# A new fixed order for the same 1440 tasks in a fused attention and MLP kernel on one core

## The chip, the core and the metric

The kernel runs on one core of a Trainium2 chip. Five engines work side by side, each through its own list of instructions in order: TensorE (PE) multiplies, with its weight loads shown as PEld; VectorE (DVE), ScalarE (ACT) and GpSimd (POOL) do the element work; SyncE (SP) issues most transfers. The metric is the device time of the kernel in microseconds, as the median of several executions. One execution is also recorded by the hardware profiler, and all durations below come from that record.

## The reference

One layer on x of shape 1 × 2048 × 640 in bfloat16: a normalisation without weights, attention with 32 heads of 20 columns over four segments of 512 tokens with a memory carried from one segment to the next, the output product and the residual, then a second normalisation and an MLP with 1728 hidden columns.

```python
q, k, v = (heads(layernorm(x) @ w) for w in (wq, wk, wv))   # B, 32, 4, 512, 20
phi = lambda t: jnp.where(t > 0, t + 1.0, jnp.exp(t))
for s in range(4):
    logits = qs @ ks.T * 20 ** -0.5 + causal_mask
    a_dot = softmax(logits) @ vs
    a_mem = (phi(qs) @ M) / (phi(qs) @ z + 1e-06)
    o = sigmoid(beta) * a_mem + (1.0 - sigmoid(beta)) * a_dot
    M = M + phi(ks).T @ vs
    z = z + phi(ks).sum(over tokens)
h = x + o @ wo
h2 = h + silu(layernorm(h) @ w1) @ w2
```

## The kernel before, in words

The 2048 tokens are sixteen blocks of 128, four blocks to a segment. Heads are taken four at a time, so a segment has eight groups, called ticks; the ticks are numbered 0 to 31 over the four segments. A function declares every piece of work as a named task with the buffers that it reads and writes. Which engine runs it, which buffer it gets and in which order the tasks are issued is then read from one long string, ORDER.

The names in ORDER, with s the segment, c a group of columns, k a tick and b a block:

- `n1_st`, `n1_rs`, `n1_ap`, `n1_tr` (b): statistics of the first normalisation on VectorE (lines 720 and 723), the reciprocal root on GpSimd (729, 731), the application on VectorE (737), the transpose by a transfer on SP (761). Blocks 0 to 3 are transposed by TensorE instead (`n1_tp`, line 746) and copied out by ScalarE or VectorE (`n1_te`, 755 and 756). `n2_` names the same for the second normalisation.
- `re_wq`, `re_wk` (c): the raw weights A_wq and A_wk copied into the column order that the heads need, in two or three pieces each, on ScalarE (693), VectorE or GpSimd (695).
- `pr` s c w: the projection for queries (w is 0) or keys (1), in two parts, `.0` with two products and `.1` with three, of 512 columns each; `qe` copies it out of PSUM (830, 831). `v` s i: the values, five products of 320 columns in each half; `ve` copies them out (797, 798).
- `ex`, `pa`, `pb`: the feature map phi (837, 844, 850). `kt`, `mz`, `ma`, `mb`: the memory's update (transpose by a transfer, products at line 1057, sum at 1083 and 1086, mask at 1093). `vt`: transfers that gather the remaining columns of the heads for groups 5 to 7.
- `qk` k with a, b or e: score products (line 900); `e` k: their exponentials on ScalarE (913), two instructions of 128 × 1024 for each; `mk` k: the causal mask on GpSimd (925). `av` k: the product with the values (948); `oe` its scaling (961, 963); `tn` k: back to token order with the memory's part (977, 981); `nm` k: the division (994 and 996, or 1008, 1013 and 1014); `ad` k: the sum of the two parts on GpSimd (1022).
- `ot` b: transpose by a transfer (1110); `wo` b: output product in two halves; `rs` b: the residual (1125). `h1_` s f: the first MLP product, again in parts with two and three products; `th` and `s`: the activation on ScalarE (1160) and VectorE (1166). `h2_` b q: the second MLP product in four parts; `o` b: the last residual (1202); `out` b: the store (1207). `x`, `w_`, `beta`: loads (578, 581, 590).
- `mt`, `mta`, `mtb`, `mm`, `mzc`, `zf`, `lsc`, `epsg`, `vpad`, `iota`, `sel`, `warm`, `fill`: constants and products that only keep TensorE busy at the start.

An entry reads `name/engine:slots`. The letter is A, D, G or S for ScalarE, VectorE, GpSimd or SyncE, where a task has a choice; `/C` on a TensorE task means that each product, whose weights are 128 columns wide, is issued as four products of 32 columns on four parts of the array (line 546 in the profile instead of 545). The array is thus used in three layouts: full (most products), four row parts (scores) and four column parts (av, `/C`, the short last part of h1). The slots are the buffers that the task takes: for TensorE tasks, PSUM banks 0 to 7, of which scores take two pairs at a time. A bank can be given anew when every task of its former owner stands earlier in the list.

A tracker then turns the list into five instruction streams. Each engine gets its own tasks in list order; semaphores are added where a task needs another engine's result, and where it writes to a buffer that another engine still has to read. So the list sets the order on every engine and also, through the slots, who waits for whose buffers. The function that reads the list:

```python
for row in ORDER:
    name, _, slots = row.partition(":")
    name, _, eng = name.partition("/")
    ...
    t.cols = eng == "C"
    t.eng = {"A": AC, "D": DV, "G": PO, "S": SP, "C": PE}[eng] if eng else list(t.engs)[0]
    ...
            a.slot = slots.pop(0)
```

Of the kernel before, what the change touches and what calls it, by code (L numbers as in the profile page):

```python
# [327 lines left out]
D = 640  # L328
# [34 lines left out]
zpad:0 iota epsc vpad1 mt0 x0:0 mta0 mtb0 halfc sel mt3 n1_st0:6 x1:1 n1_rs0 n1_st1:1 x2:2 x3:3 w_q:0 n1_st2:3 n1_rs1  # L363
n1_rs2 n1_st3:5 fill20:0 n1_rs3 re_wq0/G:0 re_wq1/G n1_ap1:0 n1_ap2:2 mm2 w_k mt1 warm:0 re_wk1/G:0 fill9:0 n1_tp1:4
mm9 re_wk2/G n1_ap0:3 n1_ap3:0 w_wv:0 n1_tp2:2 n1_tp0:0 mm6 n1_tp3:6 n1_te3/D:2 vpad0 mta3 beta n1_te1/A n1_te2/A mta1
re_wq2/G n1_te0/A re_wk0/A x4/A:4,5,6,7 mtb3 re_wk3/G pr000.0:6 pr000.1 qe000/A:0 pr010.0:1 pr001.0:2 re_wk4/A pr001.1
qe001/D pr011.0:7 pr011.1 zf0 zf1 mm8 qe011/D:0 pa011:1 re_wq3/G qk0a0:4,2 lsc0 lsc1 x8/A:8,9,10,11 ex001:1 re_wq4/G
pa001:2 pb001 kt00:0 mzc9 e0a0:4 pr010.1 qe010/D e0a2 mtb1 pr021.0:7 pr021.1 qe021/D:0 n1_st4:4 n1_rs4 v00.0:6 pa021:0
ex011:2 qk0b0:3,1 e0b0:5 e0b2 mk0b w_w1_3/S:0 w_w1_4/S pb011 v01.0:0 mm1 n1_st5:5 v00.1 ve00/A:0 pr020.0:5 pr020.1
qe020/A v01.1 n1_rs5 vt09:0 ex021:1 vt03 w_w2_5/S qk0e0:2,6 e0e2:0 v02.0:4 v02.1 v03.0:6 e0e0 n1_st6:6 ve01/D ve02/A  # L370
n1_st9:1 qk1a0:2,0 n1_ap5:2 n1_rs6 v03.1 n1_ap6:0 e1a0:1 pr031.0:4 pr031.1 kt01:1 n1_tr5:0 vt00 e1a2 n1_tr6 ve03/D
qk1b0:2,5 e1b0:6 e1b2 pb021 qe031/D:0 w_w1_0/S pr030.0:7 pr030.1 n1_ap4:3 n1_tr4 pr041.0:4 mk1a qk2a0:2,0 n1_st10:3
lsc2 mzc6 pa031:1 qe030/D pr041.1 qe041/D:0 ex031:1 pr040.0:5 pr040.1 vt06 e2a2:3 qe040/D vt08 vt04 e2a0 qk2b0:6,0
e2b0:2 vt07 lsc3 mk0e mk1b mz00:4 mk0a ma00/D:0 pb031 vt02 n1_rs10 av1:3 e2b2 oe1/D:1 mm5 mm11 mzc5 av0:2 oe0/D:0 mm0
qk2e0:4,6 e2e0:6 mz01:0 ma01/D:2 tn0:2 qk3a0:4,0 e2e2 mt2 e3a2:0 nm0:1,0 tn1:3 nm1:1 v10.0:2 v10.1 mk2b n1_st7:5
ve10/D:1 kt02:0 e3a0 mk2a n1_st11:6 qk3b0:0,6 mk2e vt05 e3b2:1 n1_rs7 e3b0 vt01 av2:5 oe2/D:1 mm3 mk3a qk4a0:6,2
mz02:4 ma02/D:3 mk3b v11.0:0 e4a2:2 vt010 e4a0 qk4b0:2,4 n1_rs9 mta2 mm4 n1_ap7:3 n1_st8:5 n1_rs8 kt03:1 e4b0:4 e4b2
vt011 v11.1 ve11/D mk4b tn2:7 nm2:1 pa041:2 mz03:6 ex041:2 qk4e0:2,0 e4e0:3 av3:7 e4e2 mk4a n1_tr7 epsg0 pr100.0/C:4
pr100.1/C ma03/D:4 oe3/D:0 qk5a0:2,6 mzc1 e5a0:5 mk4e pr110.0:5 pb041 e5a2 kt04:0 qe100/D:0 pr110.1 pr120.0:4
qe110/D:0 qk5b0:2,0 pa110:0 mtb2 av4:5 oe4/D:1 pa100:0 pr120.1/C mzc2 n1_ap10:3 n1_tr10:2 e5b2:6 qk6a0:0,6 w_w1_1/S  # L380
mz04:5 qe120/D:0 e5b0 ma04/D:1 v12.0:2 tn3:4 nm3:2 n1_ap8:1 e6a2:4 v12.1 ve12/D e6a0 tn4:7 ex100:1 pb100 nm4:2
qk6b0:4,0 pr101.0:6 e6b2:0 mk5b pr101.1 e6b0 qk6e0:0,2 e6e2:1 mk5a av5:7 n1_rs11 pa120:0 mzc0 e6e0 pr111.0/C:4 qe101/D
w_w2_3/S pr111.1/C qk7a0:2,5 e7a0:3 e7a2 n1_ap9:3 oe5/D:0 pr130.0:7 n1_tr8 qe111/D tn5:0 pa111:2 mm7 v13.0:4 nm5:2
pr130.1 qe130/D:0 qk7b0:2,0 mzc7 mzc3 mb01:0 mk6b v13.1/C ex111:1 pb111 mk6e mk6a av6:6 n1_tr9 mzc4 ve13/D e7b2:5
pr140.0/C:7 pr140.1/C qk8a0:0,4 pa101:1 oe6/D:0 pr121.0:6 pr121.1 e7b0 qe140/D:0 tn6:7 ex101:2 ex120:0 pb101 mb02:0
pb120 e8a0:4 mk7b e8a2 qk8b0:2,0 w_wo/S:0 e8b2:0 e8b0 mk7a qe121/D av7:6 nm6:0 pr131.0/C:7 oe7/D:1 kt10:1 qk8e0:0,4
e8e2:6 tn7:6 pa130:0 kt11:0 nm7:0 pr131.1/C qe131/D e8e0 mz11:2 ma11 qk9a0:5,3 mzc8 pr141.0:7 w_w2_4/S n1_ap11:3
vt10:0 mb03:0 e9a2:3 e9a0 ot0:1 mk8b mz10:1 ot1 mb00:0 ma10 pr141.1 pa121:0 mk8e qk9b0:0,2 e9b2:1 wo0.0:4 wo0.1 mk8a
av8:2 e9b0 mk9b ex131:2 qe141/D qk10a0:0,6 mk9a rs0 oe8/D:0 wo1.0:3 wo1.1 e10a0:2 e10a2 n2_st0:5 rs1 n2_st1:2 ot2
wo2.0:2 n2_rs0 ex110:0 qk10b0:0,5 e10b2:5 vt110 wo2.1 rs2 ot3 wo3.0:4 e10b0 wo3.1 pa131:2 ex121:1 qk10e0:2,0 e10e2:0  # L390
v20.0:6 v20.1 n2_rs1 n2_ap1:2 v21.0:0 e10e0 w_w1_2/S pb131 pb121 rs3 ve20/A:0 vt13 qk11a0:4,2 vt17 vt19 e11a0:4
n2_st2:1 vt15 v21.1 v22.0:6 tn8:4 e11a2 n1_tr11 n2_tr1:1 pb110 mk10a ex141:0 mk10b v22.1 w_w2_0/S n2_st3:7 n2_ap0:0
epsg1 nm8:3,1 vt16 v23.0:2 vt12 n2_rs2 ve22/A v23.1 n2_ap2:1 mk10e ve21/A ex140:2 n2_rs3 qk11b0:6,4 av9:0 ve23/D
ex130:1 e11b2:6 n2_ap3:3 oe9/D:1 av10:1 mzc11 vt14 oe10/D:0 pb130 e11b0 pr201.0/C:2 pr201.1/C qk12a0:0,4 e12a2:2
qe201/D:0 ex201:1 mk11a e12a0 mm10 tn9:6 n2_tr0 pr211.0:3 pr211.1 n2_tr2 n2_tr3 tn10:4 mzc10 mb04:0 ad8:0 nm9:3,0
qe211/A:0 nm10:0,1 vt11 pa141:1 h1_0_0_0.0:2 h1_0_0_0.1 mk11b av11:6 pa140:0 th0_0_0:0 s0_0_0:0 oe11/D:0 pb141
qk12b0:0,3 h1_0_1_0.0:7 h1_0_1_0.1 ad9 kt12:1 mz12:5 kt13:0 mz13:6 vt18 e12b2:1 tn11:2 e12b0 th0_1_0:1 vt111 ma12 ma13
qk12e0:4,0 e12e0:4 pr221.0:6 e12e2 ad10 s0_1_0 pr221.1 h1_0_2_0.0:7 h1_0_2_0.1 nm11:0,1 th0_2_0:0 qk13a0:3,1 e13a2:0
h1_0_3_0.0:5 mk12a mk12b h1_0_3_0.1 qe221/D:0 e13a0 pa211:2 pa201:0 pb201 mk12e kt14:0 mz14:6 pr231.0:2 s0_2_0 av12:7
ma14 th0_3_0:1 mk13a ex211:0 oe12/D:0 qk13b0:3,0 e13b0:2 e13b2 mk13b pr231.1 h1_0_4_0.0:6 s0_3_0 h1_0_4_0.1 th0_4_0:0  # L400
qe231/D:0 qk14a0:2,4 e14a2:1 w_w2_1/S h1_0_5_0.0:7 pb140 tn12:0 h1_0_5_0.1 e14a0 s0_4_0 pr200.0:6 pr200.1 th0_5_0:0
nm12:3,0 qk14b0:0,3 qe200/D s0_5_0 e14b0:3 av13:2 oe13/D:0 h1_0_6_0.0/C:5 h1_0_6_0.1/C qk14e0:1,6 e14b2 pr241.0:0
pr241.1 qe241/D:0 ad12 th0_6_0:1 h1_0_7_0.0:4 h1_0_7_0.1 e14e2:5 tn13:6 e14e0 s0_6_0 qk15a0:0,2 mk14b th0_7_0:0
e15a0:2 h1_0_8_0.0:5 e15a2 h1_0_8_0.1 s0_7_0 th0_8_0:0 nm13:2,0 mk14a h1_0_9_0.0:4 pb211 h1_0_9_0.1 pr210.0:7
qk15b0:0,2 mk14e av14:6 s0_8_0 pr210.1 oe14/D:1 ex200:1 e15b0:4 th0_9_0:1 s0_9_0 h1_0_10_0.0:1 kt20:0 h1_0_10_0.1
e15b2 ad13 mk15a qe210/D h1_0_11_0.0:0 qk16a0:4,2 th0_10_0:0 s0_10_0 tn14:6 nm14:1,0 h1_0_11_0.1 e16a2:0 e16a0
th0_11_0:0 h1_0_12_0.0:1 h1_0_12_0.1 th0_12_0:1 pa200:0 pb200 mk15b ad11 s0_11_0 qk16b0:6,3 e16b2:3 av15:5 oe15/D:1
pr220.0/C:2 pr220.1/C s0_12_0 e16b0 qe220/D h1_0_13_0:3 th0_13_0:0 pa221:0 s0_13_0 kt21:1 pa231:2 qk16e0:6,0 e16e0:5
tn15:4 pr230.0:2 ad14 nm15:2,0 pa210:0 pr240.0:3 e16e2 pr230.1 qk17a0:6,0 qe230/D mz20:4 mk16a mb10:0 ex221:0 ma20
e17a0:1 pr240.1/C mk16b qe240/D e17a2 mb11:0 mk16e qk17b0:4,6 e17b2:6 av16:2 ad15 mz21:3 pa240:0 oe16/D:0 mk17a  # L410
# [860 lines left out]
```

## Time and profile before

| | |
|---|---|
| median of 3 executions | 301.94 us (301.9 to 303.04) |
| the profiled execution | 301.67 us |
| its span, first to last instruction | 299.9 us |
| granted TensorE clock | 1.000 |
| TensorE matmuls busy | 284.8 us, 3134 recorded |
| VectorE, ScalarE, GpSimd busy | 222.5, 212.6, 150.0 us |
| moved by transfers | 24.68 MB, 82 GB/s over the span |

The span is what the profile covers; the execution's own time has 1.8 us more around it. A row of the profile names a line of the kernel, an engine, the tiles written and read with their shapes, the number of instructions, and their time. "Idle before" is the time in which the engine did nothing before such an instruction, with the engine or transfer whose signal came last. PSUM has eight banks in this kernel, all in one tile `ps_all`, so a wait for a bank shows under the line that emptied it. A few per cent of matmul records can be missing; the weight loads are all there, 3160 of them.

### The profile page before, as it was taken

What the parts mean: (1) busy time and instruction counts of PE and PEld (TensorE: products, weight loads), DVE (VectorE), ACT (ScalarE), POOL (GpSimd) and SP (SyncE); (2) the same over time, 40 slices, a digit from 0 to 9 for tenths busy, and PEclk for the clock granted to TensorE, in tenths of its full rate; (3) what the DMA queues carried; (4) which work ended last, traced back from release to release, by engine and by line L of the source; (5) the groups of instructions that cost most, each with busy time, mean ns of one, the idle gap of its engine ahead of it and who ended that gap; (6) DMA issues with size and microseconds to landing.
All of it is one profiled execution on the core that took longest, in us unless ns stands there. A gap on an engine that the chain in (4) does not pass through costs nothing.

```text
span 299.9 us, 7708 instructions
## 1 busy us (share of the span) xinstructions
PE 284.8 (95%) x3134; PEld 158.7 (53%) x3160; DVE 222.5 (74%) x460; ACT 212.6 (71%) x273; POOL 150.0 (50%) x299
## 2 busy tenths in 40 slices
PE   8799889989989999999999999999999999999996
PEld 5354444435545444566654454555654557764574
DVE  6498988987999868879968975698545777726622
ACT  3699999999988999975788768877888741004400
POOL 5896886674665355746563752445863621300000
PEclk9999999999999999999999999999999999999999
DMA  7787524936663103064447220601511013321021
GB/s 212 260 258 115 118 48 103 216 75 150 166 101 89 20 2 87 5 96 80 80 93 125 46 44 7 112 2 23 61 40 30 2 48 65 71 63 44 1 90 44
DMA packets 48579, 24.68 MB, mean 82 GB/s; under 512 B 38880, under 2 KB 47456, under 8 KB 48544
## 3 DMA queue, kind: packets, MB, share of 16 engines
q1 hardware_dynamic: 47488, 22.88, 35.2%
q10 hardware_dynamic: 1056, 1.31, 1.4%
q8 instruction: 25, 0.41, 0.6%
q14 instruction: 10, 0.08, 0.1%
HBM read 10.41 MB, written 2.62 MB: 43 GB/s over the span
## 4 chain that ended last, share of the span: by engine, by line
PE 70%; DVE 14%; DMA 6%; ACT 6%; issue 2%; SPq 1%; POOL 0%; DVEq 0%; ACTq 0%
PE ps_all L545 48%; PE ps_all L546 6%; PE ps_all L900 6%; PE ps_all L948 4%; ACT PT L913 4%; DMA sT<-in_A_wk_dram 3%; DVE stt L720 2%; DMA x_tok<-in_A_x_dram 2%; PE ps_all L977 2%; DVE x_tok L1125 1%; PE ps_all L1057 1%; PE ps_all L981 1%; DVE sT L1166 1%; DVE phiQ L850 1%; DVE xn_rot L737 1%
## 5 line engine op out<-in xcount | busy, mean ns | idle before, releaser
L913 ACT ACTIVATE PT<-ps_all 128x1024 bf16<-128x1024 f32 x160 | 154.9, 1028 | 27.6 <-PE ps_all L900 24.7
L925 POOL TENSOR_SCALAR_AFFINE_SELECT PT<-PT 128x512 bf16<-128x512 bf16 x128 | 82.1, 648 | 63.2 <-ACT PT L913 59.9
L1160 ACT ACTIVATE th<-ps_all 128x512 f32<-128x512 f32 (+1 forms) x56 | 32.1, 591 | 35.9 <-PE ps_all L545 28.8
L545 PE MATMUL ps_all<-tT,w_sb 128*128 128x512 bf16 x224 | 53.8, 380 | 1.5 <-issue 0.5
L545 PE MATMUL ps_all<-w_sb,sT 128*128 128x320 bf16 x376 | 53.9, 299 | 0.0
L1166 DVE SCALAR_TENSOR_TENSOR sT<-th,ps_all 128x512 bf16<-128x512 f32 (+1 forms) x56 | 36.2, 662 | 16.9 <-ACT th L1160 16.3
L545 PEld LDWEIGHTS ps_all<-w_sb,sT 128*128 128x128 bf16 x376 | 35.9, 98 | 15.6 <-issue 1.5
L545 PEld LDWEIGHTS ps_all<-tT,w_sb 128*128 128x128 bf16 x233 | 21.0, 98 | 26.1 <-issue 2.8
L720 DVE BATCH_NORM_STATS2 stt<-x_tok 128x6 f32<-128x320 bf16 x64 | 28.0, 479 | 2.2 <-DMA x_tok<-in_A_x_dram 1.8
L1202 DVE SCALAR_TENSOR_TENSOR x_tok<-ps_all,x_tok 128x640 bf16<-128x640 f32 (+1 forms) x17 | 13.2, 781 | 19.9 <-PE ps_all L545 14.7
L1022 POOL TENSOR_TENSOR otok<-on 128x320 bf16<-128x320 bf16 x24 | 19.2, 801 | 12.7 <-DVE on L1014 12.7
L545 PE MATMUL ps_all<-wv_sb,tT 128*128 128x320 bf16 x155 | 24.3, 300 | 0.2
L963 DVE TENSOR_SCALAR oTs<-ps_all,lsc 128x512 bf16<-128x512 f32 x29 | 21.4, 744 | 3.8 <-PE ps_all L948 3.5
L545 PE MATMUL ps_all<-wo_sb,tT 128*128 128x320 bf16 x160 | 23.6, 299 | 0.6 <-DMA tT<-otok 0.6
L948 PE MATMUL ps_all<-PT,Vx 128*32 128x384 bf16 (+3 forms) x512 | 22.7, 301 | 1.2 <-DVE QK L831 0.7
L831 DVE CAST QK<-ps_all 128x512 bf16<-128x512 f32 x26 | 17.8, 686 | 7.0 <-PE ps_all L545 6.9
L1014 DVE TENSOR_TENSOR on<-ps_all,rd 128x640 bf16<-128x640 f32 x24 | 19.8, 825 | 1.3 <-POOL otok L1022 0.5
L729 POOL TENSOR_TENSOR rst<-mvt,eps_c 128x1 f32<-128x1 f32 x32 | 6.6, 207 | 27.8 <-DVE mvt L723 27.7
L545 PE MATMUL ps_all<-tT,wqr 128*128 128x512 bf16 x70 | 18.1, 379 | 2.2 <-DVE tT L756 1.2
L545 PE MATMUL ps_all<-tT,wkr 128*128 128x512 bf16 x72 | 18.8, 379 | 1.3 <-issue 1.1
L731 POOL TENSOR_TENSOR rst<-rst,eps_c 128x1 f32<-128x1 f32 x32 | 18.0, 563 | 2.5
L545 PEld LDWEIGHTS ps_all<-wo_sb,tT 128*128 128x128 bf16 x160 | 15.0, 98 | 7.8 <-issue 1.1
(86 smaller groups left out, 356.4 us busy)
## 6 DMA issues: line engine op xcount, KB each, us to landing
out_dram<-x_tok SPq DMA_DIRECT2D x15, 160.0 KB, 1.9
w_sb<-in_B_w_dram SPq DMA_DIRECT2D x5, 432.0 KB, 4.0
w_sb<-in_B_w_dram SPq DMA_DIRECT2D x3, 480.0 KB, 3.9
x_tok<-in_A_x_dram ACTq DMA_DIRECT2D x2, 640.0 KB, 4.9
QKV<-QK SPq DMA_DIRECT2D x12, 72.0 KB
sT<-in_A_wq_dram SPq DMA_DIRECT2D x1, 800.0 KB, 6.2
sT<-in_A_wk_dram SPq DMA_DIRECT2D x1, 800.0 KB, 8.0
wv_sb<-in_A_wv_dram SPq DMA_DIRECT2D x1, 800.0 KB, 9.6
```

Of the source, the lines that this page charges most:

```text
L545: return [lambda e: e.matmul(out, lhsT=lhsT, rhs=rhs, start=start, stop=stop)]
L546: return [lambda e, p=p: e.matmul(out[p:p + 32, :], lhsT=lhsT[:, p:p + 32], rhs=rhs, start=start, stop=stop, tile_position=(0, p)) for p i ...
L720: T.add(DV, lambda e, hh=hh: e.bn_stats(out=stt[:, s, 6 * hh:6 * hh + 6], in_=xb[:, 320 * hh:320 * hh + 320]), reads=R((xa, xsub)), writes ...
L731: T.add(PO, lambda e: e.tensor_tensor(out=rst[:, s, :], in0=rst[:, s, :], in1=eps_c[:, 1:2], op=ALU.pow), reads=R((st, ["r"]), (C, ["half" ...
L913: T.add(AC, lambda e: e.activation(out=pt[:, pta.slot, q0:q0 + 2, 0:width], in_=sc3[:, b0:b0 + 2, 0:width], func=ACT.Exp, scale=SCALE), re ...
L925: fns.append(lambda e, v=v: e.affine_select(out=v, in_=v, pattern=[[0, 4], [1, 128]], compare_op=ALU.is_ge, fill=0.0, base=0, channel_mult ...
L948: fns.append(lambda e, j=j, r=r, h=h, pa=pa, pt=pt, co=co, q0=q0, ji=ji: e.matmul(bank(po)[32 * r:32 * r + 32, q0:hi], lhsT=Vx[:, vx.slot, ...
L963: f = lambda e: e.tensor_scalar(out=o, in0=i_, scalar1=lsc[:, g:g + 1], scalar2=None, op0=ALU.mult)
L1014: T.add(DV, lambda e: e.tensor_tensor(out=on[:, ona.slot, :, :].rearrange("p b (x e) -> p b x e", e=DH), in0=v[:, :, :, 0:DH], in1=r2.unsq ...
L1022: T.add(PO, lambda e: e.tensor_tensor(out=o_dst, in0=on[:, ona.slot, 0, :].rearrange("p (i x) -> p i x", i=4), in1=on[:, ona.slot, 1, :].r ...
L1160: T.add(AC, lambda e: e.activation(out=th[:, tha.slot, lo:hi], in_=bank(ps)[:, lo:hi], func=ACT.Tanh, scale=0.5), reads=R((ps, [0])), writ ...
L1166: T.add(DV, lambda e: e.scalar_tensor_tensor(out=sT[:, f, lo:hi], in0=th[:, tha.slot, lo:hi], scalar=1.0, in1=bank(ps)[:, lo:hi], op0=ALU. ...
```

## The change

Only the text of ORDER differs. Both strings hold 1440 entries with the same names, so no task is added or taken away, and the functions, buffers and loads are as they were. What differs is the place of entries in the list, the slots, the engine letter of 23 tasks, and the `/C` mark, which 38 tasks carry before and 43 after. The first 18 or so lines of each string, and the places that are spoken of later:

```diff
-zpad:0 iota epsc vpad1 mt0 x0:0 mta0 mtb0 halfc sel mt3 n1_st0:6 x1:1 n1_rs0 n1_st1:1 x2:2 x3:3 w_q:0 n1_st2:3 n1_rs1
-n1_rs2 n1_st3:5 fill20:0 n1_rs3 re_wq0/G:0 re_wq1/G n1_ap1:0 n1_ap2:2 mm2 w_k mt1 warm:0 re_wk1/G:0 fill9:0 n1_tp1:4
-mm9 re_wk2/G n1_ap0:3 n1_ap3:0 w_wv:0 n1_tp2:2 n1_tp0:0 mm6 n1_tp3:6 n1_te3/D:2 vpad0 mta3 beta n1_te1/A n1_te2/A mta1
-re_wq2/G n1_te0/A re_wk0/A x4/A:4,5,6,7 mtb3 re_wk3/G pr000.0:6 pr000.1 qe000/A:0 pr010.0:1 pr001.0:2 re_wk4/A pr001.1
-qe001/D pr011.0:7 pr011.1 zf0 zf1 mm8 qe011/D:0 pa011:1 re_wq3/G qk0a0:4,2 lsc0 lsc1 x8/A:8,9,10,11 ex001:1 re_wq4/G
-pa001:2 pb001 kt00:0 mzc9 e0a0:4 pr010.1 qe010/D e0a2 mtb1 pr021.0:7 pr021.1 qe021/D:0 n1_st4:4 n1_rs4 v00.0:6 pa021:0
-ex011:2 qk0b0:3,1 e0b0:5 e0b2 mk0b w_w1_3/S:0 w_w1_4/S pb011 v01.0:0 mm1 n1_st5:5 v00.1 ve00/A:0 pr020.0:5 pr020.1
...
+mt2:0 mta2 epsc zpad x0:0 mt3 iota sel fill20:0 fill9:0 n1_st0:5 x1:1 x2:2 x3:3 w_q:0 mt0 halfc mta0 n1_rs0 w_k w_wv:0 warm:0
+n1_st1:4 n1_rs1 n1_st2:2 n1_rs2 n1_st3:6 n1_rs3 mt1 re_wq0/G:0 n1_ap0:0 n1_tp0:6 n1_te0/A:2 vpad0 n1_ap1:2 n1_tp1:2
+n1_te1/A re_wk2/G:0 mta1 mta3 mtb0 n1_ap2:1 n1_tp2:0 n1_ap3:0 n1_tp3:4 n1_te2/D n1_te3/A pr000.0:0 re_wk0/D pr000.1
+qe000/D:0 re_wq1/A pr010.0:1 re_wk1/A mtb2 pr001.0:2 pr001.1 qe001/A ex001:0 re_wq2/D beta pr011.0:7 pr011.1 qk0a0:5,3
+zf0 qe011/D:0 pa001:1 zf1 pa011:2 e0a0:4 mm2 pr021.0/C:2 x4/S:4,5,6,7 pr010.1/C qe010/D e0a2 pr021.1/C pr020.0/C:5
+ex011:2 re_wk3/G qk0b0:3,0 e0b2:1 qe021/D:0 v00.0:6 v00.1 e0b0 re_wq3/G pb001 pr020.1 v01.0:0 pb011 x8/S:8,9,10,11
+kt00:1 re_wk4/G w_w1_2/S:0 ve00/A:0 qe020/A vt09:0 n1_st6:4 vt06 qk0e0:2,6 vt00 v01.1 n1_st5:2 mzc2 vt03 vpad1 pa021:0
...
```

The order on TensorE alone at the places that are spoken of later, as the two strings give it:

```diff
-qk2b0 mz00 av1 av0 qk2e0 mz01 tn0 qk3a0 tn1 v10.0 v10.1 qk3b0
+qk2b0 mz00 av0 av1 qk2e0 mz01 tn0 tn1 qk3a0 v10.0 qk3b0 v10.1/C
-av6 pr140.0/C pr140.1/C qk8a0 pr121.0 pr121.1 tn6 qk8b0 av7 pr131.0/C qk8e0 tn7
+pr140.0/C av6 qk8a0 pr140.1 tn6 pr121.0 pr121.1 qk8b0 av7 pr131.0/C qk8e0 tn7
-v20.0 v20.1 v21.0 qk11a0 v21.1 v22.0 tn8 v22.1 v23.0 v23.1 qk11b0 av9 av10
+v20.0 v20.1 v21.0 v21.1 qk11a0 v22.0 v22.1 tn8 v23.0 v23.1 av9 qk11b0 av10
```

Engines of the 23 tasks: re_wq1 and re_wk1 go from GpSimd to ScalarE, re_wq2 from GpSimd to VectorE, re_wk4 from ScalarE to GpSimd; n1_te3, qe001, ve23, qe301, qe320, qe330, ve32, ve33 and oe24 from VectorE to ScalarE; re_wk0, n1_te2, qe000, ve21, qe310, qe321, qe341 and oe25 from ScalarE to VectorE; the loads x4 and x8 from ScalarE's queue to SP's.

The last lines of the two strings:

```diff
-h1_3_13_0:5 s3_4_0 th3_9_0:1 h2_12_0:0 s3_9_0 s3_7_0 th3_10_0:1 s3_10_0 h2_12_1 h2_12_2 th3_13_0:0 s3_13_0 h2_12_3
-h2_15_0:5 o12 h2_15_1 h2_15_2 h2_15_3 o15 h2_14_0:0 h2_14_1 out12 h2_14_2 h2_13_0:2 out9 h2_14_3 h2_13_1 h2_13_2 out5
-out15 o14 h2_13_3_0 o13_0 h2_13_3_1 out14 out13_0 o13_1 out13_1
+h1_3_12_0.1 th3_7_0:0 s3_7_0 th3_10_0:0 h2_14_0:6 h2_14_1 th3_12_0:1 s3_12_0 h2_15_0:0 h2_15_1 h2_15_2 s3_10_0
+h2_12_0:4 h2_15_3 o15 out15 h2_14_2 h2_12_1 h2_12_2 h2_12_3 o12 out12 h2_14_3 o14 out14 h2_13_0:3 h2_13_1 h2_13_2
+h2_13_3_1 o13_1 out13_1 h2_13_3_0 o13_0 out13_0
```

## The prediction

> **What bounds the kernel now.** I read the busy shares first, then the forty slices, then the busy time by stage, and last TensorE's timeline in the stage where it idles.
>
> ```profile
> span 299.9 us, 7708 instructions
> PE 284.8 (95%) x3134; PEld 158.7 (53%) x3160; DVE 222.5 (74%) x460; ACT 212.6 (71%) x273; POOL 150.0 (50%) x299
> PE   8799889989989999999999999999999999999996
> DVE  6498988987999868879968975698545777726622
> ACT  3699999999988999975788768877888741004400
> PEclk9999999999999999999999999999999999999999
> ```
>
> TensorE is busy for 284.8 of 299.9 us at the full granted clock, so its idle 15.1 us is nearly all that a new order can win. The slices show that ScalarE is full only in the first third, and VectorE nearly so; the stages give the sizes (columns: PE, PEld, DVE, ACT, POOL busy, each with its count):
>
> ```profile
> 17.40:66.00 48.60, 44.12 (x559) 21.90 (x567) 43.24 (x101) 46.85 (x55) 36.35 (x83) 1.00 0.58 125
> 66.00:100.00 34.00, 31.59 (x343) 17.37 (x346) 30.40 (x64) 30.67 (x40) 18.95 (x35) 1.00 0.58 121
> 100.00:240.00 140.00, 137.46 (x1762) 75.50 (x1774) 106.41 (x215) 113.19 (x143) 76.65 (x127) 1.00 0.27 50
> 240.00:299.90 59.90, 57.15 (x390) 35.71 (x391) 31.42 (x57) 11.96 (x22) 4.88 (x11) 1.00 0.20 53
> ```
>
> From 17.4 to 66 us ScalarE is busy 46.85 of 48.60 us: the exponentials of the scores set the pace and TensorE idles 4.5 us. From 66 to 100 it idles 2.4 us, VectorE being the fuller. From 100 to 240 us TensorE is the bound (2.5 us idle), and after 240 the 2.75 us are almost all the last update and store. So only the first 100 us hold anything worth moving. What TensorE waits for there (start, length, what came next, idle before it and its releaser):
>
> ```profile
> 33.39 0.40 PE L900 MATMUL ps_all<-w_sb 20*128 20x512 bf16 x4 [0.24 <-ACT PT L913]
> 37.40 0.40 PE L900 MATMUL ps_all<-w_sb 20*128 20x512 bf16 x4 [0.56 <-ACT PT L913]
> 52.27 0.73 PE L948 MATMUL ps_all<-PT,Vx 128*32 128x512 bf16 x16 [0.22 <-DVE otok L996]
> 61.85 0.73 PE L948 MATMUL ps_all<-PT,Vx 128*32 128x512 bf16 x16 [0.69 <-DVE QK L831]
> 68.30 0.99 PE L545 MATMUL ps_all<-wo_sb,tT 128*128 128x320 bf16 x6 [0.64 <-DMA tT<-otok]
> 78.31 0.39 PE L900 MATMUL ps_all<-QK 20*128 20x512 bf16 x4 [0.34 <-DVE x_tok L1125]
> 83.11 0.40 PE L900 MATMUL ps_all<-QK 20*128 20x384 bf16 x8 [0.60 <-DVE on L1014]
> ```
>
> Six of these seven are no waits for data (the one at 68.30 is): the releaser emptied the PSUM bank that TensorE writes next. They hang on which bank a product gets and how much TensorE work stands between its two uses: just what the list fixes.
>
> **The change, part by part.** Both lists have the same 1440 entries, so no product or element operation comes or goes; only engine, bank, place and the column form (128 wide, or four times 32) differ. The sum is made against the profiled execution's 301.67 us (span 299.9 and 1.8 around it), 0.27 us under the median of 301.94.
>
> (a) The start. The first copy of A_wk (re_wk0) goes from ScalarE, where its two pieces took 0.84 us, to VectorE; the second copies of both weights go from GpSimd to ScalarE, re_wq2 to VectorE. The weight lands at 11.2 us in both. TensorE has pr000 and two products of pr010 to do until 11.97 and now starts pr001 at 12.08: 0.1 us is there to win. No bf16 copy of 400 columns on VectorE is in the trace; the nearest row is line 844 (512 columns), in two states, 15 us and 30 to 100 us into the run:
>
> ```profile
> L844 DVE TENSOR_SCALAR phiK<-w_sb x2: 403/544/684, 15.2 to 15.8; 128x512 bf16<-128x512 bf16 x2
> L844 DVE TENSOR_SCALAR phiK<-QK x7: 279/284/586, 54.9 to 96.0; 128x512 bf16<-128x512 bf16 x7
> ```
>
> Mostly 0.28 us, but 0.40 to 0.68 beside GpSimd's copies at 15.2 us. Two pieces cost 0.4 to 1.4 us, hence −0.1 to +0.5 us for the start; I take −0.1, as GpSimd's queue has only one copy there (re_wk2, 0.9 us). The Trainium skill ("SBUF — State Buffer", section "SBUF: two separate sides") says more: VectorE and GpSimd share a port pair under an exclusive lock, and the loser is blocked for the other's whole instruction. By that, re_wk0 waits out a 0.52 us copy and the term is +0.5; the lengthened row at 15.2 us agrees in direction. The loads x4 and x8 go from ScalarE's queue (0.42 and 0.37 us of issue) to SP's, behind the same wait for re_wk0; behind them on SP stand the transpose kt00 and loads issued from 16.67 us on, and SP stands idle from 5.4 us until then: nothing, and 0.8 us on kt00 (needed 15 us later) if that cover were gone.
>
> (b) Tick 0. Now qk0b0 stands behind qk0a0 and thirteen products; the new list has ten, v00.0's five being put after it and pr020's two before, so 5 × 0.157 − 2 × 0.24 = 0.3 us less. ScalarE stood idle 0.59 us for these scores, and is full from there on. −0.4 us, bounds −0.6 and 0 (then the first exponentials hold it anyway).
>
> (c) Waits that get more cover. For each bank I summed the TensorE work between its last use and the next, at the rows' pace (L545: 53.8/224 = 0.24 us a product of 512 columns, 24.3/155 = 0.16 of 320), and set it beside the emptying. av7 (61.85): its bank comes from tn6, moved ahead of pr121, instead of pr121 itself: cover 0.6 before, 1.3 now, against 0.69 for the cast. qk11a0 (78.31): v21.1 moves in front: 1.9 to 2.5. qk11b0 (83.11): av9 moves in front: 1.2 to 1.95, and its bank is released by line 1014 (0.82 us behind two short ones). mz01 and tn0, at 32.3 and 32.8 us, swap banks, so tn0 has 2.3 instead of 0.7, and the two idles of 0.18 and 0.24 us round them go. Gone: 0.69 + 0.34 + 0.60 + 0.42 = −2.05 us; bounds −2.9 (the 0.56 and 0.29 at 37.4 and 42.0, whose covers change by 0.1 and −0.35, go as well) and −1.0 (half, because full ScalarE hands the wait on).
>
> (d) New short covers: av5 1.9 to 1.3 behind line 996's pair (+0.3), tn1 now directly behind mz01 (0.33 us of copy), qk3b0 behind two of line 996, tn15 behind a cast: each 0.3 to 0.5 short on paper, of which the old list's shortfalls became idle at nearly half. +0.5 us, bounds 0 and +1.5.
>
> (e) Column form: 145 products before (580 instructions of lines 546 over 4), 158 now; 6.8/27 = 0.252 against 0.240 us: 13 × 0.012 = +0.2. Changes between the three array layouts: 180 before, 181 now; a product before scores held TensorE some 0.3 us longer than before its like: +0.2 with rounding, bounds 0 and 0.3.
>
> (f) 100 us on: as many short covers as before; 0, bounds ±1.2 (half the 2.5 idle either way). The end: the last four transposes follow 84 products (11.6 us) as before and go out 1 us later, where 2 us were spare; the last two half blocks swap; h2_13_0 takes a bank that o12 empties, with eight products as cover (1.1 against 0.82 + 0.2): 0, bounds 0 and +0.6.
>
> Sum: −0.1 − 0.4 − 2.05 + 0.5 + 0.2 + 0.2 = −1.65, so 300.0 us for the profiled execution and **300.3 us** for the median.
>
> **The rivals.**
> *Waits change place* (no change, 301.9). The exponentials pace the first 66 us; if ScalarE, at 96%, is the true bound there, TensorE's idle removed at 61.85 returns at the next scores, and only (b) is kept against (d) and (e). For: 46.85 of 48.60. Against: at 78 and 83 us ScalarE is no longer full.
> *VectorE becomes the bound* (slower, 304.4). It works in list order. Ahead of qk4a0 the new list puts n1_ap7, n1_st8, ma02 and pa041 and the moved copies, 3.4 us more; ahead of qk11a0 two statistics (2 × 1.03), ve21 (0.82), epsg1 (0.64) and the copies (1.2), with n2_ap0 (0.47) for n2_ap1 and less pb121 (0.53), 4.2 us more. In the first stage VectorE idles 5.4 of 48.6 us and absorbs it; at 66 to 90 us two slices read 9. Where the work ahead passes the idle there (34.0 − 30.4 = 3.6 us), bank releases on VectorE (lines 1014, 1125, 831) come late: it decides from about 3.6 us, and the price is the waits of (c) kept (2.05) and about 2 us more in 66 to 100. 300.3 + 2.05 + 2 = 304.4. Against: the additions at tick 11 are work that the old list runs two ticks later anyway.
> *The port lock* (300.9): term (a) +0.5, all else as forecast; that is the skill's rule just cited.
>
> **How the numbers follow.** Forecast 0.47, waits change place 0.17, lock 0.08, VectorE 0.28. A measurement of this kernel tells about 0.5% (1.5 us) from no change, so faster means under 300.4, slower over 303.4: faster 0.47, no change 0.25, slower 0.28. The forecast's own range is 298 to 300.4 from the bounds of (c), (d) and (f); with the rivals 297.6 to 304.9, leaving about a tenth on either side.
>
> **What would show it.** The idle before lines 948 at the eighth tick, and 900 at the eleventh, gone; ScalarE's 0.59 us at 17 us under 0.25; pr001 at or before 12.1 us; TensorE's idle from 14 to 100 us down from 7.0 to about 5.4 us and from 100 to 240 still 2 to 3 us. I am wrong if VectorE shows above 95% from 66 to 100 us with TensorE idle for it, or if the waits stand as long under other names, or if the 100 to 240 stage idles over 4 us, which no term here pays for.

## The result, and the profile after

| | before | after |
|---|---|---|
| median of 22 runs each | 303.02 us (301.26 to 304.43) | 301.69 us (300.21 to 305.45) |
| ratio | | 0.9957, interval 0.9939 to 0.9974 |
| the profiled execution, and its span | 301.67, 299.9 us | 301.82, 300.1 us |

The new list is faster by 0.43 per cent, 1.33 us. The two profiled executions say the contrary, by 0.15 us. That gap was the first thing to explain. In some executions the granted TensorE clock is below 1 (half for one stretch of 3.4 us in two profiles below) and the time longer, 304.4 us against 302.5 in the median for the kernel before, so the experiments give medians at the full clock as well. The top of the page of after and its stages (columns as before):

```profile
span 300.1 us, 7796 instructions
...
PE 283.6 (95%) x3174; PEld 157.9 (53%) x3199; DVE 221.2 (74%) x462; ACT 213.4 (71%) x274; POOL 148.3 (49%) x296
...
PE   6699889898989999999999999999999999999996
...
DVE  5589987977998878879978976596655866825513
```

```profile
17.40:66.00 48.60, 44.95 (x595) 21.96 (x593) 43.62 (x102) 46.95 (x57) 34.53 (x80) 1.00 0.51 115
66.00:100.00 34.00, 31.45 (x375) 17.39 (x376) 29.64 (x65) 30.63 (x40) 21.60 (x40) 1.00 0.53 116
100.00:240.00 140.00, 137.60 (x1723) 76.01 (x1734) 106.38 (x216) 114.89 (x145) 75.76 (x126) 1.00 0.31 58
240.00:300.10 60.10, 57.17 (x391) 35.20 (x391) 31.07 (x55) 11.74 (x22) 5.04 (x11) 1.00 0.22 47
```

From 17.4 to 66 us TensorE idles 3.65 us where it idled 4.48, ScalarE stays full, and VectorE has less to do from 66 to 100 us (29.64 against 30.40), not more. The first two slices of TensorE fell from 8 and 7 to 6 and 6: in this execution it begins later. What TensorE waits for on the way (its timeline; start, length, what came next, idle before it and its releaser):

```profile
35.18 0.84 PE L545 MATMUL ps_all<-wv_sb,tT 128*128 128x320 bf16 x5 [0.58 <-ACT PT L913]
...
42.33 0.29 PE L900 MATMUL ps_all<-w_sb 20*128 20x256 bf16 x4 [0.60 <-DVE Mz L1083]
...
62.60 0.73 PE L948 MATMUL ps_all<-PT,Vx 128*32 128x512 bf16 x16
...
71.63 2.21 PE L545 MATMUL ps_all<-wo_sb,tT 128*128 128x320 bf16 x15 [0.90 <-DMA tT<-otok]
...
84.64 0.40 PE L900 MATMUL ps_all<-QK 20*128 20x384 bf16 x8 [1.00 <-DVE on L1014]
```

The first line is v10.0, which now waits where it did not before. The third is av7, which had 0.69 us of idle before it and now has none. The fifth is qk11b0, whose 0.60 was to go and became 1.00. The second and fourth are waits for transfers: qk4e0 needs the last gathered columns (vt05), wo1 the transpose ot1. (At 42 us the timeline names VectorE, which had been done; in a second execution, below, the same wait is put down to the transfer.) At that product, qk4e0, the kernel before idled as well, for another reason (timeline of before), so what is new there is the difference:

```profile
41.34 0.29 PE L900 MATMUL ps_all<-w_sb 20*128 20x256 bf16 x4 [0.34 <-DVE Vx L798]
```

Between the places that the prediction named stand two waits that are new with the new list (timeline of after), the products tn5 and qk7b0:

```profile
55.37 0.33 PE L981 MATMUL ps_all<-ident,oTs 128*128 128x84 bf16 x4 [0.34 <-DVE oTs L963]
...
57.75 0.40 PE L900 MATMUL ps_all<-QKV 20*128 20x384 bf16 x8 [0.29 <-DVE otok L996]
```

The best reading is a table of segments. I followed each product through the list and took the start of a few of them as marks, chosen so that each segment holds the same products in both lists; each row is the time from the mark before, in us. "Second" is another execution of the same kernel, f1 an experiment below.

| from, to | before | before, second | after | after, second | f1 | f1, second |
|---|---|---|---|---|---|---|
| 0 to qk0a0 | 14.34 | 15.64 | 15.25 | 14.16 | 14.97 | 15.87 |
| to qk5a0 | 29.42 | 29.43 | 29.26 | 30.39 | 29.08 | 28.91 |
| to qk10a0 | 26.66 | 26.36 | 25.80 | 25.79 | 25.80 | 25.80 |
| to qk12a0 | 15.51 | 15.53 | 16.40 | 16.15 | 15.43 | 15.80 |
| to the first h1 product | 2.48 | 3.46 | 2.08 | 2.05 | 2.05 | 2.05 |
| to the last store | 209.77 | 209.91 | 209.58 | 209.47 | 209.54 | 209.38 |
| in all | 298.18 | 300.33 | 298.37 | 298.01 | 296.87 | 297.81 |

A segment in which no transfer is waited for can agree between executions of one list to a hundredth (25.80, 25.79, 25.80, 25.80). The 15.87 of f1's second execution says little of the start, since the granted clock was 0.5 from 10.4 to 13.8 us there. In the pair of first profiles the new list wins 0.16, 0.86, 0.40 and 0.19 us in four segments and loses 0.91 before tick 0 and 0.89 in the stretch of ticks 10 and 11. From qk0a0 to the last store it is 0.72 us shorter in the first pair (283.84 and 283.12) and 0.84 in the second (284.69 and 283.85).

### The profile page after: what moved, and what is told of

Its sections match the earlier page's. It is cut to its first block, busy times and chain, and to the rows that moved or that the text cites. A ratio compares the mean times of both kernels' runs of the same rounds, so it can differ in the third digit from the quotient of the medians.

```text
span 300.1 us, 7796 instructions
## 1 busy us (share of the span) xinstructions
PE 283.6 (95%) x3174; PEld 157.9 (53%) x3199; DVE 221.2 (74%) x462; ACT 213.4 (71%) x274; POOL 148.3 (49%) x296
## 4 chain that ended last, share of the span: by engine, by line
PE 68%; DVE 15%; ACT 7%; DMA 6%; issue 2%; SPq 1%; ACTq 0%
PE ps_all L545 46%; PE ps_all L546 7%; PE ps_all L900 6%; ACT PT L913 6%; PE ps_all L948 4%; DMA sT<-in_A_wk_dram 3%; DVE xn_rot L737 2%; DVE stt L720 2%; PE ps_all L977 2%; DMA x_tok<-in_A_x_dram 2%; DVE sT L1166 1%; DMA tT<-otok 1%; PE ps_all L981 1%; PE ps_all L1057 1%; DVE x_tok L1125 1%
## 5 line engine op out<-in xcount | busy, mean ns | idle before, releaser
L545 PE MATMUL ps_all<-w_sb,sT 128*128 128x320 bf16 x390 | 56.4, 300 | 0.0
L545 PE MATMUL ps_all<-tT,w_sb 128*128 128x512 bf16 x220 | 52.1, 380 | 1.4 <-issue 0.5
L545 PEld LDWEIGHTS ps_all<-w_sb,sT 128*128 128x128 bf16 x390 | 37.0, 98 | 16.0 <-issue 1.3
L545 PE MATMUL ps_all<-wo_sb,tT 128*128 128x320 bf16 x150 | 22.1, 300 | 0.9 <-DMA tT<-otok 0.9
L545 PE MATMUL ps_all<-wv_sb,tT 128*128 128x320 bf16 x145 | 22.2, 300 | 0.6 <-ACT PT L913 0.6
L545 PE MATMUL ps_all<-tT,wqr 128*128 128x512 bf16 x67 | 17.1, 380 | 1.9 <-POOL wqr L695 1.2
L545 PEld LDWEIGHTS ps_all<-wo_sb,tT 128*128 128x128 bf16 x150 | 14.0, 98 | 8.0 <-issue 1.3
```

The costliest lines, as they stand in the source:

```text
L545: return [lambda e: e.matmul(out, lhsT=lhsT, rhs=rhs, start=start, stop=stop)]
```

## The experiments

Twelve runs were made, all with lists of the same 1440 tasks. The kernel before ran beside them: 302.76 us in the median beside the first four, 302.57 beside the next four, 303.08 beside the last. Ratios are to these. At the full clock (0.998 and more, 78 of the 94 executions) these three are 302.44, 302.40 and 302.99 us, and the new lists:

| | median | at the full clock (executions) |
|---|---|---|
| after | 301.69 | 301.39 (18 of 22) |
| s1 | 303.36 | 301.95 (7 of 12) |
| s2 | 301.70 | 301.54 (11 of 12) |
| s3 | 302.55 | 302.50 (11 of 12) |
| s4 | 302.70 | 302.67 (9 of 12) |
| f1 | 300.88 | 300.61 (10 of 12) |
| f2 | 302.26 | 302.05 (8 of 12) |
| f4 | 302.17 | 302.07 (9 of 12) |
| f5 | 302.42 | 300.71 (6 of 12) |
| after, second | 301.49 | 301.42 (10 of 12) |
| f1, second | 300.85 | 300.76 (6 of 7) |
| g1 | 301.97 | 301.80 (9 of 12) |

**Old start, old front, new front.** Three splices ask which stretch holds the gain: the new list with its first 80 entries in the order of before (s1), the new list to 115 us with the old behind it (s2), and the reverse (s3).

```diff
 s1:  old list's order of the first 80 entries   + new list
 s2:  new list, 704 entries (to 115 us)          + old list
 s3:  old list, 712 entries (to 115 us)          + new list
```

> The new list with its first 80 entries put in the old list's order, engines and banks (up to, not with, qk0b0). In the new kernel's profile the first projection pr001 starts 0.90 us later than in the old one's, because the third block of x and both weights landed 0.5 to 1.0 us later. Theory 'luck': those landings vary from execution to execution and the start itself is worth 0.1 us, so this kernel is as fast as the new one (ratio to it within 0.998 to 1.002). Rival 'start': the new order of the start costs 0.7 to 0.9 us each time, so this kernel is 0.9 us faster than the new one and 2.2 us faster than the old one. In its own profile: weights landing at 11.2 us or at 12.2 us is not told apart by 'luck'; by 'start' it is 11.2.

> New list up to about 115 us (704 entries), the old one behind it. Theory 'front': the whole gain of 0.43% (1.3 us) is made by covers of PSUM banks before 100 us, so this kernel is at 0.9957 of the old one like the new one. Rival 'rear': the gain is made behind 115 us, so this kernel is at 1.000 of the old one. In its profile 'front' expects the wait of 0.69 us before the eighth tick's products with the values gone and TensorE's idle from 14 to 100 us about 6 us.

> The counterpart: old list up to about 115 us (712 entries of the new list's set), the new one behind it. 'front' expects 1.000 of the old kernel, 'rear' 0.9957 of it. In its profile the wait of 0.69 us before the eighth tick's products stands under both.

Measured: s1 303.36 us, ratio 1.0005 (0.9977 to 1.0034); s2 301.7, 0.997 (0.9943 to 0.9997); s3 302.55, 0.9995 (0.9971 to 1.0019). So what gain there is sits ahead of 115 us, and the new tail brings none that can be measured. By the median of s1 the old start would give all of it back, which neither of its two expectations said; at the full clock it is 301.95 us, 0.5 under the kernel before and 0.6 over the new list. The profile of s1 shows no slow start: its qk0a0 came at 14.27 us, a whole microsecond ahead of after's, and TensorE then stood at two transfers:

```profile
42.18 0.29 PE L900 MATMUL ps_all<-w_sb 20*128 20x256 bf16 x4 [1.53 <-DMA QKV<-w_sb]
...
72.19 2.21 PE L545 MATMUL ps_all<-wo_sb,tT 128*128 128x320 bf16 x15 [1.61 <-DMA tT<-otok]
```

0.60 and 0.90 in after have become 1.53 and 1.61 (timeline of s1). The lead of 0.98 us went into the first wait, so that qk8a0 came at 59.82 against 59.97, and the second wait was longer by 0.7 for no reason that the list gives.

**The cover of av7.** In s4 tn6 goes back behind pr121, with the banks that the old list gave the two.

```diff
-pr140.1 tn6:6 pr121.0:7 pr121.1
+pr140.1 pr121.0:6 pr121.1 ... tn6:7
```

> The new list with tn6 behind pr121 again and the old list's banks for tn6, pr121 and av7, so that av7 writes to the bank that the cast qe121 empties. Theory 'cover': 0.6 to 0.7 us of idle come back before av7 and the kernel is 0.6 us slower than the new one. Rival 'waits change place': ScalarE paces this stage, so the idle comes back before av7 and goes from the next scores; time within 0.2 us of the new one.

Measured: 302.7 us, 1.0004 (0.9976 to 1.0031). The timeline of s4:

```profile
63.68 0.73 PE L948 MATMUL ps_all<-PT,Vx 128*32 128x512 bf16 x16 [1.14 <-DVE QK L831]
```

The wait is back, 1.14 us long, and from qk8a0 to qk9a0 s4 takes 6.87 us where after takes 5.79. s4 is 0.15 us ahead of after at qk8a0, 0.94 behind at qk9a0 and still 0.85 behind at the last store (299.22 against 298.37). So the removed idle was not merely handed on, although ScalarE is busy 96 per cent of the stage from 17.4 to 66 us; *waits change place* falls at this spot.

**Three repairs of the new list.** The profile of after suggests three moves: ot1 ahead of ot2 (f1), the second normalisation's n2_ap3 and n2_ap2 behind nm8 on VectorE (f2), and these two with the gathers vt010 and vt05 ahead of the transpose kt03 (f4). f5 is f4 with the old start of s1.

```diff
 f1: -ot0 ot2 mzc6 e9a2 ot1          +ot0 ot1 ot2 mzc6 e9a2
 f2: -n2_ap3 ... n2_ap2 ... nm8      +nm8 n2_ap3 n2_ap2
 f4: f1, f2, and  -vt04 kt03 ... vt010 ... vt05   +vt04 vt010 vt05 kt03
```

> The new list with one entry moved: ot1 ahead of ot2, so that SP issues the transposes for the output product in the order in which wo0, wo1, wo2 use them. In all four profiles with the new front TensorE idles 0.67 to 1.61 us before wo1 for a transfer, and never in those with the old front. Theory 'new wait': that idle is a price of the change that the forecast left out; without it the kernel is 0.6 to 0.9 us faster than the new one (0.9932 to 0.994 of the old kernel), and no idle stands at line 545 <- DMA near 72 us. Rival 'pinned later': VectorE's queue, which releases the bank before qk11b0, sets that point anyway; the idle moves to 84 us and the time stays at 0.9957.

> The new list with n2_ap3 and n2_ap2 put behind nm8 on VectorE, nothing else. The new kernel idles 1.00 us before qk11b0 because nm8 stands behind two applications of the normalisation on VectorE. 'VectorE's order': the idle goes and the kernel is 0.6 to 1.0 us faster than the new one. Rival: the two transposes behind n2_ap2 and n2_ap3 are then late for h1_0_0, whose idle takes its place; time unchanged within 0.3 us.

> The new list with three repairs: ot1 ahead of ot2, nm8 ahead of n2_ap3 and n2_ap2, and the transfers vt010 and vt05 ahead of kt03 on SP (the score product of tick 4's shared part waits 0.60 us, and 1.53 us with the old start, for the last of them). If the three waits are independent, 0.7 + 0.8 + 0.5 = 2.0 us off the new kernel, 0.989 of the old one. If each is handed on to the next, under 0.7 us. It is also the candidate to beat both kernels.

> The same three repairs on the new list with the old start. The old start had a lead of 1.0 us at tick 1 over the new one in the profiles and lost it at the wait for the gathering transfers (1.53 us) and at wo1 (1.61 us), both pinned by transfers, and so was no faster in the end. If that is why, the lead now stays: 0.5 to 1.0 us faster than the list with the repairs and the new start. If the start's times are luck, the two are equal within 0.3 us.

Measured: f1 300.88 us, 0.9948 (0.9923 to 0.9974); f2 302.26, 0.9992 (0.9967 to 1.0016); f4 302.17, 1.0 (0.9977 to 1.0023); f5 302.42, 0.9967 (0.9937 to 0.9998). In f1 the wait at ot1 is gone, ticks 10 and 11 take 15.43 us instead of 16.40, and the rows behind are as they were: in this profile all of it reaches the end. In f1's second profile 0.29 us of the wait are left (15.80 in the table): there ot1 landed 4.3 us after its issue, in the first 2.7. So the place in the queue is one part of that wait, and the time to landing another, which differed between two executions of one list. In f2 the wait before qk11b0 is gone too, and here is what comes of it (timeline of f2, first TensorE, then VectorE):

```profile
82.17 0.40 PE L900 MATMUL ps_all<-QK 20*128 20x384 bf16 x8
...
85.27 0.40 PE L900 MATMUL ps_all<-QK 20*128 20x512 bf16 x4 [0.96 <-DVE oTs L963]
```

```profile
81.02 0.82 DVE L1014 TENSOR_TENSOR on<-ps_all,rd 128x640 bf16<-128x640 f32 x1
81.76 1.80 DVE L737 TENSOR_SCALAR xn_rot<-x_tok,mvt,rst 128x640 bf16<-128x640 bf16 x2
83.48 0.41 DVE L850 TENSOR_TENSOR phiQ<-phiQ,ex 128x512 bf16<-128x512 bf16 x1
83.81 1.40 DVE L963 TENSOR_SCALAR oTs<-ps_all,lsc 128x512 bf16<-128x512 f32 x2
```

The normalisation (line 1014) started at 83.76 us in after, 4.3 us behind qk11a0, and here at 81.02, 3.0 behind it. But the two applications that stood ahead of it now stand ahead of the scaling at line 963, and qk12a0 waits 0.96 us for that. From qk11a0 to qk12a0 f2 takes 7.21 us, after 7.25. VectorE is busy 6.91 of these 7.25 us in after, and this change of its order moves the idle without removing it. The profiled execution of f2 has the shortest span of all, 298.4 us, while its median is no better than that of before: it is the fastest of the twelve, with qk0a0 at 14.11 us and no transfer waited for at 41 us. In f4 the gathers' wait shrinks, and idle reappears 1.7 us on (timeline of f4):

```profile
42.20 0.29 PE L900 MATMUL ps_all<-w_sb 20*128 20x256 bf16 x4 [0.24 <-DVE Vx L798]
...
43.89 1.02 PE L545 MATMUL ps_all<-tT,wqr 128*128 128x512 bf16 x4 [0.63 <-issue]
```

0.24 + 0.63 us for the 0.60 of after. The second row counts four of five products, so about 0.2 of its 0.63 us is the missing record of the first. It reads transposed rows (tT) whose transfer, issued behind kt03 at 40.07 us, landed at 43.59; in after it was issued at 40.22 and landed at 42.91. In f5, the slowest of its twelve executions, 2.83 us were idle there, labelled as kt03's transpose, and 1.7 us behind that wait, from 45.5 to 48.9 us, the granted clock was 0.5. Neither expectation of f2 or of f4 came true: both ratios are above the new list's 0.9957, by 0.35 and 0.43 per cent (the interval of f2 still overlaps), though from qk0a0 to the last store their profiles are shorter (282.57 and 282.81 us). That gap stays open.

**The same kernels a second time.** Two lists whose profiles agree and whose medians don't: either the first profiles are not typical, or the medians are disturbed. So both ran again, f1 too, and f1 with the old start (g1).

> The kernel before, unchanged, profiled a second time on another chip. Theory (its first profiled execution had early landings): the records of instructions agree, what differs hangs on transfers; the weights of tick 0 land more than 0.2 us later than the 8.98 and 11.19 us of the first, or a wait for a transfer inside ticks 3 to 11 is longer by 0.5 us or more, and the span is 300.5 to 301.3 us instead of 299.9. Rival (the first profile is typical and the 22 and 35 later runs were disturbed otherwise): landings within 0.2 us, span 299.7 to 300.2.

> The changed kernel, unchanged, profiled and timed a second time. Theory: the first profile's landings of 10.0 and 12.2 us for the weights of tick 0 were late ones; here they come 0.3 to 1.0 us earlier and the first projection, at 12.98 us before, with them, but the wait for the last gathered transfer at 42 us grows by about the same, so that the span is 299.5 to 300.1; ratio to before 0.994 to 0.998. Rival (the start is late by the list, the forecast -0.1 had the wrong sign): weights again at 10.0 and 12.2, first projection at 12.8 to 13.1. In both the waits of 0.9 us for the output-weight transpose and of 1.0 us behind the normalisation at 84 us stand where they stood.

> The new list with the second output-weight transpose ahead of the third, a second time, now beside the new list on the same chip. Theory (the list's order of three transposes costs 0.9 us at 71.6 us, and nothing behind takes it back): 0.7 to 1.0 us under the new list, ratio to before 0.993 to 0.996. Rival (the first measurement of 0.9948 was chance; the queue serves whichever comes first and a later wait takes the gain): within 0.3 us of the new list.

> The new list with the second output-weight transpose ahead of the third, and its first 80 entries in the order of the list before. Theory (a lead at the start is lost where TensorE waits for transfers whose issue the SP queue fixes, at 42 and at 71 us; with the second wait removed, half of it can remain): 0.0 to 0.5 us under f1. Rival (the new start is worth what the timed first pair said, some 0.4 per cent): 0.8 to 1.5 us over f1.

Measured: before 303.79 us in the one run, span 302.1; after 301.49, 0.9946 (0.992 to 0.9971); f1 300.85, 0.9922 (0.9888 to 0.9957); g1 301.97, 0.9963 (0.9937 to 0.9989). The second profile of before (copies on ScalarE, then TensorE):

```profile
12.49 0.83 ACT L693 ACTIVATE wkr<-sT 128x400 bf16<-128x400 bf16 x2 [2.68 <-DMA sT<-in_A_wk_dram]
```

```profile
90.44 1.24 PE L545 MATMUL ps_all<-tT,w_sb 128*128 128x512 bf16 x5 [1.29 <-DVE rd L1013]
```

In the first profile TensorE waited less before the same product:

```profile
88.44 1.24 PE L545 MATMUL ps_all<-tT,w_sb 128*128 128x512 bf16 x5 [0.31 <-DVE rd L1008]
```

A_wk landed at 12.5 us instead of 11.2, and all of the 1.3 us are still there at qk8a0. At 90 us, ahead of the first MLP product, TensorE idles 1.29 us for a result whose named engine had been done 0.7 us before (line 1013 ran from 89.42 to 89.77); the fifth transpose of normalised rows, issued at 85.8, would land at 90.1 with the slowest landing of that line, 4.3 us (in the first profile 88.1, 0.3 ahead of the product there). That this is the true releaser is worked out, not shown. The second profile of after (timeline, VectorE then TensorE):

```profile
10.55 0.70 DVE L695 COPY wkr<-sT 128x400 bf16<-128x400 bf16 x2 [0.74 <-DMA sT<-in_A_wk_dram]
```

```profile
42.37 0.29 PE L900 MATMUL ps_all<-w_sb 20*128 20x256 bf16 x4 [1.73 <-DMA QKV<-w_sb]
```

And the same product in f2, whose list is the new one up to there:

```profile
40.96 0.29 PE L900 MATMUL ps_all<-w_sb 20*128 20x256 bf16 x4 [0.37 <-DVE Vx L798]
```

Here A_wk was there by 10.55 us, qk0a0 came 1.09 us ahead of after's first, and the wait at 42 us grew by 1.13. The two executions of after resume at 42.33 and 42.37 us. So the first expectation holds in the main: before's first profile was an early one (10 of 116 runs of before took 301.67 us or less), though the second span, 302.1 us, is above the 300.5 to 301.3 expected. And in this execution the new list did not keep its early start. It is no rule of the list: s2 (qk0a0 at 14.38 us) keeps half of its lead over after to qk5a0, and f2 (14.11) all of it, 1.13 us at qk0a0 and 1.37 at qk5a0. Put early beside early and late beside late: before 298.18 and after, second, 298.01; before, second, 300.33 and after 298.37. The new list wins 0.2 us in the one pair and 2.0 in the other, and the medians, 1.3 to 1.6 apart, lie between.

g1 was to be 0.0 to 0.5 us under f1 and came 1.1 over it: that expectation failed, and the rival's 0.8 to 1.5 came. Its scores at tick 0 came at 15.47 us, among the late ones, and it idled 1.39 us at 43 us. What the old start costs with the new list stays open: s1 against after and g1 against f1 say 1.7 and 1.1 us (0.6 and 1.0 at the full clock), f5 against f4 says a gain of 0.3 per cent (1.4 us at the full clock). The profiles show no loss behind it but the longer waits for transfers. The granted clock may be a part: it was below 0.998 in 14 of the 36 executions of s1, f5 and g1, in 6 of 34 of the new list and 16 of 94 of the kernel before. That long waits bring it on, as f5's profile suggests, is not shown.

f1 has the lowest median of all lists: in two series 300.88 and 300.85 us, 0.5 to 0.8 per cent under the list before. Beside the new list on the same chip it is 0.64 us faster; in the first series the ratios, 0.9948 and 0.9957, differ by 0.3 us, and the intervals overlap in both. At the full clock f5 equals it (300.71 against 300.61). From qk0a0 to the last store its two profiles take 281.90 and 281.94 us, the two of before 283.84 and 284.69.

## Why the prediction was right or wrong

Two steps failed: the base, which put the absolute time 1.1 us too low, and term (c), of whose −2.05 us only −0.63 came, because it took the emptying of a bank as given; with it went the waits for transfers, which no term held.

**The base.** The sum was made against 301.67 us and the median of three runs, 301.94. That was the step that put the absolute time wrong: the median of 116 runs of before, over four series, is 302.84 us. The forecast change was −1.65 us, the measured ones −1.33 (ratio 0.9957) and −1.6 (0.9946); 300.3 us missed by 1.4 because it started 0.9 to 1.1 too low. The time lies in the range with the rivals and outside the forecast's own 298 to 300.4, whose upper end is the border of half a per cent and not the sum of the bounds: those of (c) and (d) alone reach 1.05 and 1.0 us above the forecast. The first ratio is within the half per cent that was called no change, the second just beyond it. Behind the nearly right size stand terms that were wrong one by one:

**(a) The start, −0.1.** Right, where it can be measured: in the stretch behind the landing. From the landing of A_wk to pr001 the old start took 0.88 to 0.89 us in the three executions in which TensorE waited for it (b2, g1 and f5), the new one 0.76 to 0.77 (after, f1, f4): −0.12. VectorE's two pieces took 0.71 us where ScalarE's took 0.83. *The port lock* falls as a price, +0.5, and not as a mechanism (line 695 in after; wkr beside GpSimd's copies, wqr a microsecond later without them):

```profile
L695 DVE COPY wkr<-sT x2: 285/395/505, 12.2 to 12.4; 128x400 bf16<-128x400 bf16 x1, 128x240 bf16<-128x240 bf16 x1
L695 POOL COPY wkr<-sT x2: 382/484/587, 12.2 to 12.8; 128x400 bf16<-128x400 bf16 x1, 128x240 bf16<-128x240 bf16 x1
L695 DVE COPY wqr<-sT x2: 240/288/335, 13.4 to 13.7; 128x400 bf16<-128x400 bf16 x1, 128x240 bf16<-128x240 bf16 x1
```

The 505 ns are VectorE's shorter piece, of 240 columns, which alone takes 240. In all eight profiles with the new start it ends 0.09 us behind the end of GpSimd's first piece (12.92 and 12.83 us in after), so it looks held until then, and 0.27 us dearer; VectorE's longer piece started 0.03 us ahead of GpSimd's and was not held. By the rule of the Trainium skill ("SBUF — State Buffer", section "SBUF: two separate sides"), VectorE would have been blocked for GpSimd's whole copy, if its own ran in a 2-port mode, which no run tells. The trace agrees as far as the shorter piece goes, and at half the price of the rival. What was not foreseen is that the landing itself differs by 2.2 us between executions (10.3 to 12.5), far more than the term; "pr001 at or before 12.1 us" was no test of the list.

**(b) Tick 0, −0.4.** Right. From qk0a0 to qk0b0 it is 2.60 us in every profile of after and f1, 3.02 before. It is a move, v00.0 going behind; that it is kept shows from qk0a0 to qk5a0, where both lists hold the same products: without the idle just before qk4e0, before takes 29.08 and 29.09 us there and after 28.66 in both profiles. ScalarE's idle at 17 us, 0.59 before, is 0.15 (from 17.51 + 0.63 to 18.29), as stated (first before, then after):

```profile
17.84 1.94 ACT L913 ACTIVATE PT<-ps_all 128x1024 bf16<-128x1024 f32 x2 [0.59 <-PE ps_all L900]
```

```profile
18.29 1.94 ACT L913 ACTIVATE PT<-ps_all 128x1024 bf16<-128x1024 f32 x2
```

**(c) More cover, −2.05.** This is the step that failed in size: −0.69 − 0.34 + 0.40 = −0.63 us came of it. av7's 0.69 went, as s4 confirms, and qk11a0's 0.34. But qk11b0's 0.60 became 1.00. I counted the TensorE work between two uses of the bank and took the emptying as given; the emptying, line 1014, now starts at 83.76 us behind two applications of the second normalisation on VectorE. That is the rival *VectorE becomes the bound* in small, at one tick of the stage for which it was argued, and the reordering of f2 does not remove it there. The 0.42 around mz01 and tn0 came back as 0.28 and 0.58 under other names at 34 and 35 us. In the stage from 14 to 100 us, TensorE's idle fell from 7.04 to 6.21 us instead of 5.4, and from 6.36 to 6.00 in the second profiles, in which no matmul record is missing.

**What no term held.** Two losses. SP's queue now issues ot2 ahead of ot1, and wo1 waits 0.64 to 0.90 us for it; f1 undoes most of that, 0.3 to 0.7 us in the medians. (wo0's wait of 0.64 in before, called a wait for data and not costed, is gone in return, and so is a wait that the prediction's lines left out, 0.53 and 0.20 us before mz11 for the transpose kt11.) And the last gather is 0.6 to 1.7 us late for qk4e0 at 42 us in the two profiles of after, where before idles 0.34. One gain: ahead of the first h1 product before idles 0.31 us in the one execution and 1.29 in the other, after in neither. All in all the list is worth 0.72 and 0.84 us behind qk0a0 in the two pairs of profiles, and with the start's 0.12 some 0.8 to 1.0, about half of the forecast. That the medians fell by 1.3 to 1.6, near its 1.65, is to that extent luck; where the rest comes from is not shown.

**(d), (e), (f).** New short covers, +0.5: too small. The idles at 34 and 35 us are of that kind (tn1, and the values behind it), so (c)'s 0.42 and this term are one and the same place; with the 0.34 and 0.29 at tn5 and qk7b0 they make 1.5 us, the upper bound. Against that went idles for which the sum had no gain, above all 0.56 before qk4a0. Columns and layouts, +0.4: the stretch behind the first h1 product, where little waits, is 0.2 to 0.5 us shorter with the new list, so no run shows the price. The "0.3 us longer" before scores was a misreading: the scores start 312 ns behind a product's start there, its like follows after 216, so a change costs 0.1. From 100 to 240 us TensorE idles 2.4 us, 2 to 3 as stated (1.1 before and 1.0 after in the second profiles, where no record is missing), and (f)'s 0 stands within those 0.5.

**The rivals.** *Waits change place* came true at single spots (qk12a0 in f2, tn1) and false at av7. *VectorE becomes the bound* is refuted as a whole: 29.64 of 34 us, no slower kernel.

## What to carry to other kernels

Check whether the profiled execution is typical before summing against it: here one landing, 1.3 us early or late, was as large as the whole change, and only a second profile of the same kernel showed it. When a list is reordered, follow the in-order transfer queue with the same care as the engines: one transpose issued a place too late left TensorE idle for 0.64 to 0.90 us, as much as the best covered bank gained. And cover for a bank is worth only as much as the order on the engine that empties it lets it be; sum both sides.

## What the runs showed that had not been expected

The same weight load, issued at the same place, landed from 10.3 to 12.5 us over fourteen executions of one core's program. Such a difference can last (before: 1.30 us at qk0a0, 1.31 at qk8a0), and a later wait for a transfer can swallow it (after: 1.09 us at qk0a0, −0.03 at qk8a0). In the second execution of after the gathers on SP had been issued 1.05 us earlier than in the first and were waited for until the same 42.3 us. In f2 the last of them was issued 0.11 us earlier still, and its product started at 40.96 us. What holds them in the one and not in the other is open.
